# Keeping a V tile whole, and not half of it, in SBUF between two attentions, with half-slot passing of weights and x added by a matmul

## The chip, the cores and the metric

One core of one Trainium2 chip runs the kernel; the other cores are idle. The metric is the device time of one execution in microseconds (us). "Time" below is the median of several executions. The "span" of a profile is shorter (180.4 us where the time was 182.13 us), because the time also holds start and end of the execution. PE is the matrix engine (TensorE), DVE the vector engine, ACT the scalar engine, POOL GpSimd.

## The reference, cut to what matters

Two attention layers and two feed-forward layers alternate, and both attentions use the same weights and the same caches:

```python
x = A_x                                                     # 4 x 1 x 512
x = x + _A_ref(_layernorm(x), A_k_cache, A_v_cache, A_wq, A_wo)
x = x + _B_ref(_layernorm(x), B_w_gate, B_w_up, B_w_down)
x = x + _A_ref(_layernorm(x), A_k_cache, A_v_cache, A_wq, A_wo)
x = x + _B_ref(_layernorm(x), B_w_gate, B_w_up, B_w_down)
# _A_ref: 32 query heads, 8 kv heads of 128, batch 4, softmax over the last
#         2048 of 8192 cache positions
# _B_ref: sigmoid(x @ w_gate) * (x @ w_up) @ w_down, hidden size 1792
```

All data is bf16. One V tile of 1 MiB holds the window of one kv head for two of the four batches, so there are 16 V tiles. SBUF cannot hold everything until the second attention, so most V tiles, the q weights and the feed-forward weights are read again. What stays need not be read.

## The kernel before: the parts that matter here

SBUF is an arena of slots; a 1-MiB tile takes two neighbouring slots, a half tile takes one. All big transfers are issued by one engine (SyncE, "SPq" in the profile) in one fixed order. Each is issued when its slot is free: from a pool, or from a fixed "home", a half slot of a tile that has been used up. `done` marks the last use of a tile and starts whatever transfer can then go.

```python
homes = {}; hfree = set(); on_free = {}
X = ("V", HKV - 2, 1, 0)        # kv head 6, batch pair 1, first layer
Y = ("V", HKV - 1, 0, 0)
Z = ("V", HKV - 1, 1, 0)
GA = ("wg", 0, 0)               # the gate tiles of the first feed-forward
GB = ("wg", 1, 0)

def can_take():
    name = loads[0][0]
    if name in homes:
        return all(n in base for n, _ in homes[name]) and hfree.issuperset(home(name))
    return bool(pool.free)

def done(name):
    left[name] -= 1
    if left[name] == 0:
        s = where.pop(name)
        if name in on_free: on_free[name](s)
        else:               pool.release(s)
        fill()              # issue what can go now
# ... cut ...
def load_v(h, bp, k, n_use):
    name = ("V", h, bp, k)
    if k == 1 and (h, bp) == (HKV - 2, 1):      # only its second half is read again
        load_half(name, pair_d(A_v, h, bp)[:, :, SLOT:2 * SLOT], "bw_4k", SLOT, (X, 1))
        del on_free[name]
        return
    load(name, n_use, "bw_8k", (2 * SLOT, pair_d(A_v, h, bp), True))
    if k == 1 and (h, bp) == (HKV - 2, 0):
        homes[name] = [(Y, 0), (Y, 1)]
```

`pair_d(A_v, h, bp)` is the window of one V tile in HBM. `load_half` fills one slot with rows of 4096 B, `load` two slots. In the second attention the heads run from 7 down to 0. The order of the big transfers around it is: up and down weights of the first feed-forward, the q weights once more, the half V tile, V(6,0), V(5,1), V(5,0), and so on. I call V(6,0), V(5,1) and V(5,0) the **first, second and third V tile of the second attention**. V(7,0) and a half of V(7,1) wait in PSUM in between ("stash").

## Time and profile before

| what | value | read as |
|---|---|---|
| time | 182.08 us (181.89 to 182.09, 3 runs) | |
| span of the profile | 180.4 us | |
| DVE busy | 58% | no compute engine is near the bound |
| PE busy | 56% | |
| ACT, POOL busy | 18%, 12% | |
| big transfer queue | 71.31 MB, 96.7% of 16 engines | the transfers nearly fill the span |

Sixteen transfer engines share each transfer, so the row of DMA shares is a mean over them. A mean of 1.0 over 2 us is read as nobody having waited (the share comes out above 1 in places, so small steps in it mean little).

### The profile page before, as it was taken

What the parts mean: (1) busy time and instruction counts of PE and PEld (TensorE: products, weight loads), DVE (VectorE), ACT (ScalarE), POOL (GpSimd) and SP (SyncE); (2) the same over time, 40 slices, a digit from 0 to 9 for tenths busy, and PEclk for the clock granted to TensorE, in tenths of its full rate; (3) what the DMA queues carried; (4) which work ended last, traced back from release to release, by engine and by line L of the source; (5) the groups of instructions that cost most, each with busy time, mean ns of one, the idle gap of its engine ahead of it and who ended that gap; (6) DMA issues with size and microseconds to landing.
All of it is one profiled execution on the core that took longest, in us unless ns stands there. A gap on an engine that the chain in (4) does not pass through costs nothing.

```text
span 180.4 us, 3873 instructions
## 1 busy us (share of the span) xinstructions
PE 101.6 (56%) x1639; PEld 54.9 (30%) x1651; DVE 104.4 (58%) x257; ACT 32.7 (18%) x87; POOL 21.3 (12%) x86
## 2 busy tenths in 40 slices
PE   0535326572825518335356658354977997667743
PEld 0102111342411514213226542231323443426311
DVE  7208997758474494663745564124589999531431
ACT  2002031221030300302003001001225545410101
POOL 6000010100010100101001000000013435322000
PEclk9999999999999999999999999999999999965555
DMA  5999999999999999999999999999999999999970
GB/s 188 421 429 425 423 423 414 416 423 416 421 414 423 416 423 421 414 420 425 408 420 421 409 403 403 415 352 414 391 400 429 430 412 427 414 414 407 413 312 16
DMA packets 12514, 71.57 MB, mean 397 GB/s; under 512 B 1224, under 2 KB 1232, under 8 KB 6096
## 3 DMA queue, kind: packets, MB, share of 16 engines
q1 hardware_dynamic: 12488, 71.31, 96.7%
q8 instruction: 13, 0.21, 0.5%
q14 instruction: 5, 0.04, 0.1%
q10 hardware_dynamic: 8, 0.00, 0.0%
HBM read 71.31 MB, written 0.00 MB: 395 GB/s over the span
## 4 chain that ended last, share of the span: by engine, by line
DMA 47%; PE 21%; DVE 21%; SPq 4%; ACT 3%; issue 3%; DVEq 0%; ACTq 0%
DMA arena<-in_A_v_cache_dram 31%; DVE arena L818 11%; DMA arena<-in_B_w_down_dram 9%; PE ps L847 8%; DMA arena<-in_A_wq_dram 5%; PE ps L935 5%; SPq L398 4%; PE ps L836 3%; DMA arena<-in_B_w_up_dram 3%; DVE nmax L858 2%; ACT prow L888 1%; ACT prow L873 1%; PE ps L1122 1%; PE ps L1016 1%; DVE ebuf L893 1%
## 5 line engine op out<-in xcount | busy, mean ns | idle before, releaser
L818 DVE STREAM_TRANSPOSE arena<-arena 128x1024 f32<-128x1024 f32 x32 | 37.0, 1203 | 0.0
L847 PE MATMUL ps<-arena,qbd 128*32 128x512 bf16 x256 | 25.8, 539 | 0.0
L935 PE MATMUL ps<-ebuf,arena 128*128 128x8 bf16 x576 | 17.8, 168 | 9.5 <-DMA arena<-in_A_v_cache_dram 5.4
L836 PE MATMUL ps<-msk_m,msk_s 128*32 128x512 bf16 x64 | 8.6, 527 | 23.0 <-DVE arena L818 21.8
L858 DVE TENSOR_REDUCE nmax<-ps 128x1 f32<-128x512 f32 x16 | 10.8, 676 | 17.6 <-PE ps L847 17.6
L935 PEld LDWEIGHTS ps<-ebuf,arena 128*128 128x128 bf16 x576 | 16.8, 104 | 11.6 <-DMA arena<-in_A_v_cache_dram 6.5
L873 ACT ACTIVATE prow<-ps,nmax 128x512 bf16<-128x512 f32 x16 | 11.0, 688 | 35.1 <-DVE nmax L870 29.5
L811 ACT CAST qbd<-ps 128x256 bf16<-128x256 f32 x16 | 5.9, 370 | 44.3 <-PE ps L847 34.8
L759 PE MATMUL ps<-arena,xn 128*4 128x512 bf16 x64 | 8.3, 572 | 6.6 <-DMA arena<-in_A_wq_dram 6.1
L847 PEld LDWEIGHTS ps<-arena,qbd 128*32 128x32 bf16 x256 | 8.5, 122 | 10.7 <-issue 7.8
L902 POOL CAST s<-psm 128x1 bf16<-128x1 f32 x9 | 1.7, 189 | 83.9 <-ACT prow L873 83.9
L888 ACT CAST prow<-ps 128x512 bf16<-128x512 f32 x16 | 9.4, 587 | 10.7 <-PE ps L935 2.1
L893 DVE STREAM_TRANSPOSE ebuf<-prow 128x256 f32<-128x256 f32 x16 | 7.0, 438 | 4.2 <-ACT prow L888 4.1
L836 PEld LDWEIGHTS ps<-msk_m,msk_s 128*32 128x32 bf16 x64 | 1.8, 101 | 23.8 <-DVE arena L818 19.0
L1288 PE MATMUL ps<-arena,xn 128*4 128x448 bf16 x64 | 7.2, 559 | 3.3 <-DMA arena<-in_B_w_up_dram 2.3
L1016 PE MATMUL ps<-arena,ebuf 128*32 128x512 bf16 x112 | 8.1, 413 | 1.2 <-DMA arena<-in_A_v_cache_dram 1.0
L772 DVE STREAM_TRANSPOSE ebuf<-ps 128x512 f32<-128x512 f32 x3 | 2.2, 718 | 11.2 <-PE ps L759 11.1
L806 PE MATMUL ps<-qh,eyew 32*128 32x64 bf16 x64 | 5.6, 217 | 5.0 <-ACT qbd L811 2.4
L737 ACT ACTIVATE lnv<-ps 128x4 f32<-128x4 f32 x4 | 0.7, 174 | 41.7 <-PE ps L733 41.7
L943 DVE TENSOR_TENSOR onb<-ps,rinv 128x16 bf16<-128x16 f32 x9 | 1.7, 185 | 10.7 <-PE ps L935 10.7
L1122 PE MATMUL ps<-onp,arena 128*128 128x16 bf16 x144 | 5.3, 175 | 2.4 <-DVE onp L958 2.4
L1026 DVE STREAM_TRANSPOSE arena<-ps 128x512 f32<-128x512 f32 x7 | 4.8, 692 | 2.8 <-PE ps L1016 2.8
(107 smaller groups left out, 128.1 us busy)
## 6 DMA issues: line engine op xcount, KB each, us to landing
arena<-in_A_v_cache_dram SPq DMA_DIRECT2D x29, 1024.0 KB, 21.2
arena<-in_A_k_cache_dram SPq DMA_DIRECT2D x16, 1024.0 KB, 25.2
arena<-in_A_wq_dram SPq DMA_DIRECT2D x6, 1024.0 KB, 9.3
arena<-in_A_wo_dram SPq DMA_DIRECT2D x4, 1024.0 KB, 25.0
arena<-in_B_w_gate_dram SPq DMA_DIRECT2D x4, 896.0 KB, 17.3
arena<-in_A_wq_dram SPq DMA_DIRECT2D x4, 512.0 KB, 9.3
arena<-in_B_w_up_dram SPq DMA_DIRECT2D x4, 448.0 KB, 7.1
arena<-in_B_w_up_dram SPq DMA_DIRECT2D x2, 896.0 KB, 24.2
```

The source lines that it names most:

```text
L398: o = P.op("sync", name, 0.0, lambda e, dst=dst, src=src: e.dma_start(dst, src), r=r, w=w, dma_bytes=nbytes, dma_rate=tm[rate])
L759: last = pe.matmul(ps[32 * hh:32 * hh + NB, qb, :], xn[:, c * NB:(c + 1) * NB], src[:, o + hh * 512:o + (hh + 1) * 512], start=(c == 0), s ...
L818: P.op("vector", "T%d_%d" % (h, t), c_dve(1024), lambda v, v32=v32: v.transpose(v32, v32), r=[("slot", 4 * h + t)], w=[("slot", 4 * h + t)])
L836: last = pe.matmul(ps[32 * gi:32 * gi + 32, bank, :], msk_s[:, :], msk_m[:, :].unsqueeze(1).broadcast_to([128, 256, 2]), start=True, stop= ...
L847: last = pe.matmul(ps[32 * gi:32 * gi + 32, bank, :], qbd[:, q0:q0 + 32], kt[:, cp // 2, cp % 2, jh * NJ:(jh + 1) * NJ, :], start=False, s ...
L858: lambda v: v.tensor_reduce(nmax[:, k2:k2 + 1], ps[:, bank, :], AXX, ALU.max),
L873: lambda a: a.activation(prow[:, :].rearrange("p (m x t) -> p m x t", x=32, t=2), ps[:, bank, :].rearrange("p (m t x) -> p m x t", x=32, t ...
L888: P.op("scalar", "pc" + tag, c_act(512), lambda a: a.copy(prow[:, :], ps[:, pb, :]), r=[("ppb", pb)], w=[("prow",)], banks=(pb,))
L893: P.op("vector", "pt" + tag, c_dve(256), lambda v: v.transpose(et, prow[:, :].bitcast(F32)), r=[("prow",)], w=[("e", k2)])
L935: last = pe.matmul(ps[:, ob, bp * 8:bp * 8 + 8], src[:, j * 128:(j + 1) * 128], ev[:, j % 2, j % 16 // 2, x0:x0 + 8], start=(j == 0), stop ...
L1016: last = pe.matmul(ps[32 * g:32 * g + 32, ob, :], ew[:, g, mq, t], src.rearrange("p (m t d) -> p t m d", t=2, d=128)[:, t], start=(n == 0) ...
L1288: last = pe.matmul(ps[32 * g:32 * g + NB, gub[n], 0:NF], xn[:, c * NB:(c + 1) * NB], slot_ap(s)[:, g * NF:(g + 1) * NF], start=(c == 0), s ...
```

## The change

The intent is to read 512 KB less. The other half of V(6,1) stays too, so nothing of that tile is read again. The price is room: one slot fewer is free in the feed-forward part. So the homes are shared out anew: the gate tiles GA and GB give their room in halves, the down weights come in four pieces (three of 512 KB, one of 256 KB), and the q weights go where gate tiles and V(7,0) were. The core of the diff (`...` marks what is cut):

```diff
-        X = ("V", HKV - 2, 1, 0)
...
-                    load_half(("wq", c, k), ..., ((X, 1), (Y, 0), (Y, 1), (Z, 0))[c])
+                    load_half(("wq", c, k), ..., ((Y, 1), (Z, 0), (GA, 0), (GA, 1))[c])
...
-                    homes[name] = [((GA, GB)[cc], 0), ((GA, GB)[cc], 1)]
+                    homes[name] = [((GB, Y)[cc], 0), ((GB, Y)[cc], 1)]
...
-                        load_half((nm, c, k), src[:, c, :], "bw_3k", F, ((X, 1), (Y, 0), (Y, 1), (Z, 0))[c])
+                        load_half((nm, c, k), src[:, c, :], "bw_3k", F, ((Y, 0), (Y, 1), (Z, 0), (GA, 0))[c])
...
-            if k == 1 and (h, bp) == (HKV - 2, 1):
-                load_half(name, pair_d(A_v, h, bp)[:, :, SLOT:2 * SLOT], "bw_4k", SLOT, (X, 1))
-                del on_free[name]
-                return
             load(name, n_use, "bw_8k", (2 * SLOT, pair_d(A_v, h, bp), True))
             if k == 1 and (h, bp) == (HKV - 2, 0):
-                homes[name] = [(Y, 0), (Y, 1)]
+                homes[name] = [(GA, 0), (GA, 1)]
...
+        stay = keep[1:] + [(HKV - 2, 1)]
```

Further parts: the input x is put into the PSUM bank of the wo sums by one fp32 matmul with an identity (before, DVE added it after the sum); eight q matmuls go in front of the first scores of the second attention (`score(0, lambda: q_mms(1, 0, OBS[1], (0, 1)))`); in the last attention unit one group of wo matmuls moves and the sums use another bank.

## The prediction

> **What bounds the kernel now.** I read four views of the kernel before, in this order. First the page's slices, because a kernel that streams 71 MB once is suspected of being limited by its transfers (each character or number is one fortieth of the span, 4.51 us):
>
> ```profile
> DMA  5999999999999999999999999999999999999970
> GB/s 188 421 429 425 423 423 414 416 423 416 421 414 423 416 423 421 414 420 425 408 420 421 409 403 403 415 352 414 391 400 429 430 412 427 414 414 407 413 312 16
> ...
> q1 hardware_dynamic: 12488, 71.31, 96.7%
> ```
>
> The reader is to see that the transfer engines are busy in every slice but the first and the last two, at 403 to 430 GB/s with two dips (352 and 391, slices 27 and 29). No compute row is near that (the page gives DVE 58% and PE 56%). Second, the chain of work that ended last:
>
> ```profile
> DMA 47%; PE 21%; DVE 21%; SPq 4%; ACT 3%; issue 3%; DVEq 0%; ACTq 0%
> ```
>
> DMA has the largest share but not all of it, because the chain walks from a transfer back to the compute that freed its room. So the third question is whether the room comes in time. The trace has for each transfer the time of its issue and of its landing. Before each issue between 80 and 135 us there were still 3 to 6 transfers in flight, worth 3.9 us or more of streaming: the half V tile went out at 120.67 us when the transfer before it landed at 128.75; the next V tile but one at 128.52 us against 132.69. A transfer on an idle queue took 4.98 us to land (first wq tile, 0.79 to 5.77 us), of which 1 MiB at the later spacing of landings, 2.48 us, leaves about 2.5 us of lead. So the waits of the queue for compute (27.6 us in the longest group of the view of the queue's own waits) cost nothing: they are the throttle of a full pipe. The two dips aren't starvation either: in windows of 2 us the transfer engines stay busy while the packets become slow.
>
> ```profile
> 116.00:118.00 2.00, 0.68 (x23) 0.60 (x24) 0.00 (x0) 0.00 (x0) 0.00 (x0) 1.00 1.03 377
> 118.00:120.00 2.00, 1.20 (x25) 1.03 (x22) 0.60 (x4) 0.00 (x0) 0.00 (x0) 1.00 0.96 307
> 120.00:122.00 2.00, 1.50 (x10) 0.59 (x10) 0.36 (x2) 0.00 (x0) 0.00 (x0) 1.00 1.02 414
> ```
>
> The last two columns are the DMA share and GB/s. Fourth, the timeline of the end, to see whether transfers or compute set it:
>
> ```profile
> 170.76 0.92 PE L1288 MATMUL ps<-arena,xn 128*4 128x448 bf16 x8
> ...
> 173.01 0.92 PE L1288 MATMUL ps<-arena,xn 128*4 128x448 bf16 x8 [1.33 <-DMA arena<-in_B_w_up_dram]
> ...
> 175.47 1.02 PE L1331 MATMUL ps<-arena,hT 128*4 128x128 bf16 x32 [1.12 <-DMA arena<-in_B_w_down_dram]
> 176.70 1.02 PE L1331 MATMUL ps<-arena,hT 128*4 128x128 bf16 x24 [0.20 <-DMA arena<-in_B_w_down_dram]
> ```
>
> In the last feed-forward part PE waits 1.33 us for the second up tile, then for each down tile; the last lands at 177.29 us, and the 3.1 us from there to the end of the span (last matmuls, casts, store) are fixed. So the time is: start of the stream, bytes over rate, fixed tail.
>
> **What the Trainium skill says.** "DMA: Bandwidth & Descriptors", section "Where 436 GB/s comes from", puts the fabric's ceiling at 435 GB/s; the slices here top out at 430, so there is no idle bandwidth to win, only bytes. The same page's "Rules for kernel authors" ask for 1 MiB per DMA. Half slots break that rule, but with several transfers queued the trace shows little harm: a packet of 8192 B took 311 ns in the median, one of 4096 B 159 ns, one of 6144 B 239, one of 2048 B 84. "TensorE: Matmul & The Clock Gate", "What's actually happening", says that an array that was not busy lately runs at half clock; the trace agrees: the 16 score matmuls took 1.92 us at 126.55 us and 1.11 us at 137.46. "PSUM — Partial Sum Buffer", "The four PSUM rules", says that only the first matmul of a group may clear the bits that make the others accumulate; that fits the diff, in which x's matmul opens the bank and the first wo matmul no longer does. No time follows from it.
>
> **The change, part by part.** I compared instruction order and waits of both programs on every engine.
>
> (1) The half V tile (512 KB) of the second attention is no longer read: 128 rows of 4096 B over 16 engines are 8 packets each, 8 x 159 ns = 1.27 us. The same from the rate: 0.524 MB / 414 GB/s = 1.27 us. This is on the path, since the pipe is full.
>
> (2) The down weights' third piece (768 KB, rows of 6144 B) becomes 512 KB and 256 KB: 159 + 84 - 239 = 4 ns a row, 8 rows an engine, +0.03 us. The number of transfers is the same.
>
> (3) Room comes later for several transfers. Putting the times of the kernel before on the new releasers: the third up tile now waits for the second stash transpose, about 106.9 us (issued at 104.74 before), where the transfer ahead of it lands at 111.05; the fourth for the first gate matmuls, about 108.9, against 112.19; the last wq tile for the first matmuls on the new q weights, about 120.7, against some 126; the next V tile for the third group of those, about 124.2, against some 128.7; the next for q matmuls at about 127, against some 131. The smallest lead is 3.3 us, above the 2.5. Cost 0.
>
> (4) x by a matmul. One GpSimd select and one fp32 matmul go in front of the first q matmuls. They wait for the select, about 6.8 us in place of 5.81; the first two groups of 1.02 us together still end before the second wq tile is there (8.25 us). Cost 0. In return the addition after the reduce (0.18 us, DVE) goes; but the gate matmuls after it wait for the second gate tile (landed 108.81) anyway. Gain 0.
>
> (5) Second attention. The two halves put aside in PSUM come back (2 x 0.73 us) while the last q weights are still streaming, not after; that is no longer in front of the first scores. Instead eight q matmuls (about 1.0 us at the slow clock) go in front of them and wait for a wq tile that landed at 126.13. I get the first scores at 127.2 us where they were at 126.55, the second scores at 130.1 (129.96), and the transpose of the first probabilities at 133.15 (132.89): compute runs 0.3 us later through the second attention. It has slack: the up wait above is 1.33 us. With the second up tile 1.24 us earlier (171.73) and PE free at 171.68 + 0.3, hT is ready at about 173.9, and the first down tile lands at 174.2. Cost 0.
>
> (6) In the last unit the sums move to another bank and one group of wo matmuls moves back in order, so the first PV half need not wait for a reciprocal (162.65 us). The path there is the GpSimd product ending at 163.42, so gain 0.
>
> Sum: -1.27 + 0.03 = -1.24 us, 182.08 - 1.24 = 180.84, rounded to **180.8 us** (-0.7%).
>
> **The rivals.** (A) Compute of the second attention becomes the bound, and part of the gain stays in a shorter wait. For it: its units follow one another every 3.3 us without waiting for V tiles until 153.96 us, and my working leaves 0.3 us of slack at the first down tile. Against: behind that tile lies more slack, because the three groups of down matmuls need 1.8 us and are spread over 2.3 by their tiles; compute must be about 1.1 us late to cost anything. At its likely worst, another 0.5 us: 181.3. (B) The queue starves in the feed-forward part, as a whole slot less is free there. For it: the lead of 3.3 us is the smallest of the kernel, and one engine may run ahead of the others. Against: the rate at the smallest leads of before (4 transfers in flight at 104 us) was 404 GB/s, no dip. It would cost up to 1 us: 181.8. (C) The dips (about 1 us of bytes together, worked out from the windows) come from the order of the transfers and change with it. They have no releaser, so I can't tell which way: 180.0 to 181.7. (D) The bytes are hidden anyway and nothing is gained, 182.1: I see no place in which the pipe is empty, so unlikely.
>
> **Range and chances.** The centre is 180.8. (C) and the spread of the runs (181.89 to 182.09) give 0.5 either way; (A) and (B) only lengthen, so the range is 180.2 to 181.5. Faster by over 2% means under 178.4 us, which needs twice the bytes saved: 0.01. Slower by over 2% means over 185.7, which needs a starved queue of 5 us: 0.01. Within 2%: 0.98.
>
> **What would show it right or wrong.** Right: bytes of the big queue fall to 70.8 MB, slices stay at 400 to 430 GB/s through the feed-forward part, the last down tile lands near 176.05 us, and the wait for the second up tile shrinks from 1.33 us to almost nothing (step 5). Step 3 is wrong if a new dip comes with a DMA share under 0.9 between 108 and 135 us. Step 5 is wrong if the down matmuls wait for hT and not for a transfer. Step 4 is wrong if a q matmul before 10 us starts after its tile by more than it does now. The whole is wrong if the stream is as long as before with fewer bytes.

## The result

The changed kernel took **182.08 us** (181.92 to 182.33, 4 runs), the kernel before in the same rounds 181.99 us (181.41 to 182.09, 4 runs). The outputs are right. The ratio is 1.0013, with a 95% interval of 0.9988 to 1.0037. A ratio is the mean time of one kernel's runs over that of the other's of the same rounds, so it is not quite the ratio of the medians quoted. The 0.52 MB are gone and the time is the same; the prediction of 180.8 us (180.2 to 181.5) missed.

The page of the kernel after, in the slices of one fortieth of the span, the big queue, and the engines' shares of the chain that ended last:

```profile
DMA  5999999999999999999999999999999999999970
GB/s 192 416 429 427 422 425 411 416 422 420 420 414 424 414 424 420 416 416 424 412 417 427 406 402 384 411 331 420 369 393 418 424 425 420 418 411 404 418 292 11
...
q1 hardware_dynamic: 12488, 70.79, 96.5%
...
DMA 36%; DVE 32%; PE 21%; SPq 4%; issue 3%; ACT 2%; POOL 1%; DVEq 0%; ACTq 0%
```

The bytes fell as foreseen, from 71.31 to 70.79 MB. The share of the queue hardly moved, so the packets of fewer bytes took nearly as long. The slices 25, 27 and 29 fell from 403 to 384, from 352 to 331 and from 391 to 369 GB/s. Transfers lost 11 points of the chain to DVE, and the chain through DVE is work whose end frees room for a transfer.

The timeline of the end in the kernel after (start and duration in us, then the releaser and the idle time before):

```profile
170.56 0.92 PE L1295 MATMUL ps<-arena,xn 128*4 128x448 bf16 x8 [0.82 <-DMA arena<-in_B_w_up_dram]
172.83 0.92 PE L1295 MATMUL ps<-arena,xn 128*4 128x448 bf16 x8 [1.35 <-DMA arena<-in_B_w_up_dram]
...
175.32 1.02 PE L1338 MATMUL ps<-arena,hT 128*4 128x128 bf16 x32 [1.14 <-DMA arena<-in_B_w_down_dram]
176.57 1.01 PE L1338 MATMUL ps<-arena,hT 128*4 128x128 bf16 x24 [0.23 <-DMA arena<-in_B_w_down_dram]
```

It is the picture of before, 0.1 to 0.2 us earlier: PE still waits 1.35 us for the second up tile, and then for the down tiles. So compute is not the bound. The last landing came at nearly the same time (177.16 us against 177.29), though the stream had less to carry: it must have been slower, or idle, somewhere.

The windows of 2 us at the entry of the second attention show where. First the kernel before, then the kernel after (the window, its length, busy time and count for PE, PE weight loads, DVE, ACT and POOL, the granted clock, the DMA share, GB/s):

```profile
126.00:128.00 2.00, 1.85 (x20) 0.68 (x20) 0.81 (x2) 0.26 (x1) 0.00 (x0) 1.00 1.04 406
128.00:130.00 2.00, 2.00 (x28) 0.69 (x24) 1.34 (x5) 0.37 (x1) 0.00 (x0) 1.00 1.03 412
130.00:132.00 2.00, 1.88 (x20) 0.52 (x13) 2.00 (x5) 0.78 (x2) 0.00 (x0) 1.00 0.93 348
132.00:134.00 2.00, 1.83 (x32) 0.72 (x32) 1.50 (x3) 0.86 (x2) 0.54 (x2) 1.00 1.00 418
```

```profile
118.00:120.00 2.00, 1.15 (x14) 0.91 (x14) 0.80 (x6) 0.00 (x0) 0.00 (x0) 1.00 1.04 274
...
126.00:128.00 2.00, 2.00 (x24) 0.81 (x27) 0.00 (x0) 0.37 (x1) 0.00 (x0) 1.00 1.09 387
128.00:130.00 2.00, 2.00 (x24) 0.56 (x16) 0.56 (x1) 0.25 (x1) 0.00 (x0) 1.00 0.94 369
130.00:132.00 2.00, 2.00 (x20) 0.44 (x16) 1.86 (x7) 0.91 (x3) 0.00 (x0) 1.00 0.85 344
132.00:134.00 2.00, 1.42 (x28) 0.67 (x29) 1.90 (x5) 0.86 (x2) 0.54 (x2) 1.00 0.97 401
```

From 126 to 134 us the kernel before moved 406, 412, 348 and 418 GB/s, the kernel after 387, 369, 344 and 401. That is 83 GB/s less over 2 us, or 0.17 MB of the 0.52 MB saved. Between 130 and 132 us the DMA share is 0.85: engines were idle, which is the sign that the prediction had named for its step 3. Already before, that window had 0.93, which the prediction did not look at; but a second trace of the kernel before (run e6_before_again) has no dip there:

```profile
130.00:132.00 2.00, 1.39 (x28) 0.59 (x21) 1.97 (x5) 1.17 (x3) 0.00 (x0) 1.00 1.00 401
```

The changed kernel shows it in both its traces (0.89 and 356 GB/s in e0_after_again). The dip at 118 to 120 us (307 GB/s before, 274 after) has a share of 0.96 and 1.04, so there the packets were slow and almost nobody waited.

### The profile page after: what moved, and what is told of

Read it like the earlier page. It is cut to its first block, busy times and chain, and to the rows that moved or that the text cites. A ratio compares the mean times of both kernels' runs of the same rounds, so it can differ in the third digit from the quotient of the medians.

```text
span 180.3 us, 3876 instructions
## 1 busy us (share of the span) xinstructions
PE 101.7 (56%) x1641; PEld 54.9 (30%) x1653; DVE 104.3 (58%) x256; ACT 32.7 (18%) x87; POOL 21.5 (12%) x87
## 3 DMA queue, kind: packets, MB, share of 16 engines
q1 hardware_dynamic: 12488, 70.79, 96.5%
## 4 chain that ended last, share of the span: by engine, by line
DMA 36%; DVE 32%; PE 21%; SPq 4%; issue 3%; ACT 2%; POOL 1%; DVEq 0%; ACTq 0%
DMA arena<-in_A_v_cache_dram 20%; DVE arena L819 11%; DMA arena<-in_B_w_down_dram 9%; PE ps L848 7%; DMA arena<-in_A_wq_dram 5%; PE ps L938 5%; DVE nmax L861 4%; SPq L398 4%; DMA arena<-in_B_w_up_dram 2%; PE ps L837 2%; DVE arena L1027 2%; DVE ebuf L896 2%; DVE nmax L865 2%; DVE mxt L869 2%; DVE arena L1032 1%
## 5 line engine op out<-in xcount | busy, mean ns | idle before, releaser
L1019 PE MATMUL ps<-arena,ebuf 128*32 128x512 bf16 x112 | 7.5, 385 | 0.2 <-DVE nmax L873 0.2
L1306 DVE STREAM_TRANSPOSE ebuf<-ps 128x448 f32<-128x448 f32 x4 | 2.6, 651 | 7.1 <-PE ps L1295 7.1
```

Source lines behind the costliest of these rows:

```text
L1019: last = pe.matmul(ps[32 * g:32 * g + 32, ob, :], ew[:, g, mq, t], src.rearrange("p (m t d) -> p t m d", t=2, d=128)[:, t], start=(n == 0) ...
```

## Reading the stream engine by engine

A mean share does not tell which engines wait. The trace has sixteen completions for each transfer, one of each engine. From these I worked out, for each transfer, the time between one completion and the next, place by place in the order of arrival (first engine with first engine, and so on). For the second V tile of the second attention, which takes 2.48 us an engine in a full pipe, in us:

```
before   3.20 3.16 3.09 3.08 3.04 2.98 2.90 2.88 2.57 2.93 2.48 2.48 2.49 2.49 2.48 2.46
after    3.05 2.92 2.94 2.93 2.91 3.01 2.79 2.79 2.76 2.74 2.69 2.79 2.76 3.09 3.21 3.36
```

In the kernel before the first ten places lost up to 0.7 us on this tile, and the six last lost nothing. The landing, which is the last engine's, showed a clean 2.5 us. So in this execution the stage was already short of work before the change, and the view by landings hid it. In the second trace of the same kernel the loss is small (2.57 us in the mean, 2.76 at most): the kernel before stood at the edge.

The reason is that the sixteen engines are not in step. In the kernel before, the first transfers of the program arrive on all engines within 0.39 us. In the transfer that streams from 30 to 34 us the spread becomes 1.53 us, and it does not close again (1.4 to 3.0 us from there to the end). At 30.8 us the trace has one packet of 16,384 B of the instruction queue, which took 1.08 us on one engine. This fits the size of the jump; the profile does not say which engine carried it. The trace of the kernel before has thirteen such packets of 0.88 to 1.11 us, and the five 1-MiB tiles that stream when one is carried at 43.5, 59.8, 72.1, 85.7 and 99.0 us took 2.57 to 2.60 us in the mean of the engines, the other 1-MiB tiles in rows of 8192 B of that stretch 2.45 to 2.52. My estimate from these numbers, 2.49 us plus a sixteenth of 1.08, is 2.56.

**The account.** The mean completion over the sixteen engines is a steadier clock for the account than the last one, though the time itself follows the last: in all 14 traces the profiled execution took 4.83 to 4.95 us more than its last landing. Three things came out of the mean. (a) From the end of the third V tile of the second attention on, the rest of the stream took 38.56 to 38.74 us in all 14 traces, so everything is decided before. (b) The last big transfer completed at 175.53 us (mean of engines) in the kernel before, at 175.60 in a second trace of it, and at 175.14, 174.91 and 175.22 us in three traces of the changed kernel or one of the same order of transfers. That is 0.48 us earlier in the mean, where 1.27 were removed. (c) The three V tiles together took 7.83 and 7.63 us before and 8.37, 8.34 and 8.40 after, which is 0.64 us more. The last up piece took 1.13 and 1.15 us before and 1.34, 1.34 and 1.21 after, 0.16 us more. The down pieces of the first feed-forward took 4.47 and 4.88 us before and 4.54, 4.53 and 4.81 after, so 0.05 us less in the mean, which is nothing beside their scatter. And -1.27 + 0.64 + 0.16 - 0.05 = -0.52, near the measured -0.48. So 0.8 us of the 1.27 were lost in two places, and the larger is the entry of the second attention.

## The experiments

Three theories went into the runs. **S**: at the entry of the second attention the transfers wait for compute to free their room; the engines that are ahead run dry, and removing bytes in front of such a wait only makes the wait longer. **P**: the loss is in slow packets (as at 118 us) and in the chance of which engine ends last. **C**: compute is the bound. The runs came in three calls, each on another chip; those of one call share the runs of the kernel before. Its times were 181.61 us (181.06 to 182.53, 11 runs) in the first call, 182.0 (181.61 to 182.84, 11) in the second and 181.83 (181.32 to 182.45, 11) in the third.

| run | time, us (range, runs) | ratio to before [95%] | three V tiles, us | mean end of stream, us |
|---|---|---|---|---|
| e6_before_again | 181.76 (181.37 to 182.01, 4) | 0.9978 [0.9948, 1.0007] | 7.63 | 175.60 |
| e0_after_again | 181.3 (181.07 to 182.97, 6) | 1.000 [0.996, 1.0039] | 8.34 | 174.91 |
| e1_bytes_alone | 181.87 (181.54 to 182.35, 6) | 1.001 [0.9983, 1.0038] | 8.77 | 174.90 |
| e2_more_room | 180.56 (180.17 to 181.13, 6) | 0.9938 [0.991, 0.9965] | 7.55 | 173.75 |
| e2_more_room_again | 180.44 (180.25 to 180.84, 4) | 0.9917 [0.989, 0.9944] | 7.61 | 174.16 |
| e7_room_and_bytes | 181.74 (181.56 to 182.46, 6) | 0.9988 [0.996, 1.0015] | 7.54 | 175.20 |
| e3_bytes_back | 182.21 (181.47 to 182.85, 6) | 1.0025 [0.9993, 1.0057] | 7.62 | 176.29 |
| e4_halves | 181.13 (180.3 to 181.76, 6) | 0.9943 [0.9914, 0.9971] | 8.32 | 174.58 |
| e4_halves_again | 181.3 (180.44 to 181.53, 6) | 0.9958 [0.9934, 0.9982] | 7.92 | 174.51 |
| e8_more_halves | 180.97 (180.38 to 181.97, 6) | 0.9958 [0.9927, 0.9988] | 7.80 | 174.51 |
| e5_scores_first | 181.52 (180.97 to 182.85, 6) | 0.998 [0.9945, 1.0015] | 8.14 | 174.87 |
| e9_x_by_vector | 181.76 (181.17 to 182.63, 4) | 0.9997 [0.9965, 1.0028] | 8.40 | 175.22 |

The last two columns are of the one profiled execution of each run, the times of all.

### The same kernels again: what a run scatters

No edit in either: e0 is the changed kernel, e6 the kernel before.

> The changed kernel unaltered, for a second trace and a tighter interval. Theory S (starved queue: with less room the transfers into the second attention are issued too late, so the engines idle and the saved 1.27 us are lost there): 181.7 to 182.3 us, with idle of the DMA engines again between 130 and 135 us and again between 110 and 115. Theory P (packets happened to be slow in the one trace, at 117 to 120 and 126 to 128 us, and one engine lagged at the end): the median comes nearer to 181.3 and the slow spells move or vanish in the second trace.

> The kernel before unaltered, for a second trace. All theories: ratio 1.00 within 0.4%. Theory S: again some idle between 130 and 135 us, about 0.2 us an engine, less than the changed kernel has.

The changed kernel gave 1.000, the unchanged one 0.9978 against itself. The median of the changed kernel, 181.3 us, is the figure that P had named, but the kernel before was faster in this call too (181.61), so the ratio counts, and it shows no gain. The idle of S is there again (a share of 0.89 from 130 to 132 us). So a single ratio of some six runs is good to about 0.3% or 0.5 us, and the missing gain of 0.7% is more than that. The account by engines, which does not depend on the end, is steadier: the three V tiles took 8.37 and 8.34 us in the two traces of the changed kernel.

### The bytes alone

The kernel before, with the load of the half V tile replaced by nothing. Half of V(6,1) is then stale, so the result is wrong, though within the tolerance.

```diff
-                load_half(name, pair_d(A_v, h, bp)[:, :, SLOT:2 * SLOT], "bw_4k", SLOT, (X, 1))
-                del on_free[name]
+                left[name] = 1
+                homes[name] = [(X, 1)]
+                loads.append((name, lambda s: None))
```

> The kernel before with the half V tile simply not read (wrong result on purpose, everything else as before). If the stream is bound by bytes, it is 1.27 us faster: 180.7. Theory S: the next V tile but one is still issued when the first scores are done, about 128.5 us, and the tile ahead of it now lands about 131.4, a lead of 2.9 us for its last engine and under 1 us for its first; the engines idle there and only 0.2 to 0.8 us are gained, 181.2 to 181.8. Theory P: 180.7 or what the slow packets leave.

The ratio was 1.001 [0.9983, 1.0038]: with everything else as before, 512 KB less in the stream gained nothing that these runs can see, where 0.7% was the price of the bytes. S had expected 0.2 to 0.8 us of gain. The windows of this run:

```profile
126.00:128.00 2.00, 1.73 (x20) 0.70 (x20) 0.93 (x2) 0.37 (x1) 0.00 (x0) 1.00 1.06 420
128.00:130.00 2.00, 2.00 (x32) 0.75 (x28) 1.24 (x4) 0.37 (x1) 0.00 (x0) 1.00 0.69 289
130.00:132.00 2.00, 1.67 (x29) 0.49 (x18) 1.98 (x5) 1.25 (x3) 0.00 (x0) 1.00 0.82 311
132.00:134.00 2.00, 1.56 (x30) 0.53 (x22) 1.86 (x6) 0.39 (x2) 0.53 (x2) 1.00 0.97 381
```

The DMA share falls to 0.69 and 0.82. Here the idle time stands in the open: the second V tile was issued at 128.64 us, as in the kernel before (128.52), because its room is freed by score matmuls, and those do not come sooner for there being fewer bytes. The first engine had done with the first V tile at 129.20 us, 0.6 us after that issue. The second tile then took 4.12 us in the first place of the order of arrival in place of 2.48, and 2.77 in the last. In the mean the three tiles took 8.77 us against 7.73, so 1.04 of the 1.27 us was lost there. This is S in its plainest form. (The stream of this trace still ended 0.7 us earlier than before, because the q weights ahead took 10.44 us and not 10.92; the traced execution, 181.56 us, was nearly the fastest of the six, whose median was 181.87.)

### More room, the same bytes

The changed kernel, but V(6,1) is not kept, nor read again: V(6,0) is used in its place, so the result is wrong. The slots that V(6,1) held go to the pool. The first V tile takes those, and the second V tile takes the home that the first had.

```diff
-            if k == 1 and (h, bp) == (HKV - 2, 0):
+            if k == 1 and (h, bp) == (HKV - 3, 1):
                 homes[name] = [(GA, 0), (GA, 1)]
...
-        stay = keep[1:] + [(HKV - 2, 1)]
+        stay = keep[1:]
...
+            if h == HKV - 2:
+                v_tiles[(2, h)] = [(bp, ("V", h, 0, 1)) for bp in range(2)[::-1]]
...
-                if (h, bp) not in keep + stay:
-                    load_v(h, bp, 1, 1)
+                if (h, bp) not in keep + stay + [(HKV - 2, 1)]:
+                    load_v(h, bp, 1, 2 if (h, bp) == (HKV - 2, 0) else 1)
```

> The changed kernel with its bytes but one whole slot more room: the second V tile of head 6 isn't kept (its place goes to the pool, and the second attention reads the other tile twice; wrong result on purpose). V tiles are issued one slot earlier. Theory S: the idle at 130 to 135 us vanishes, 0.4 to 1.0 us faster than the changed kernel, 181.1 to 181.7. Theory P: no difference to the changed kernel beyond 0.2 us.

> The same kernel as e2_more_room, to see how far a ratio moves from call to call, and to set e4_halves and e8_more_halves beside the kernel that has room in plenty on the same chip. Theory S: ratio 0.992 to 0.995, the best of this call or equal to e8_more_halves. Theory P: ratios of all kernels move toward 1.0.

The ratios were 0.9938 and 0.9917. With the bytes of the changed kernel and two slots more, the gain is there: the mean of the two is 0.9928, or 1.3 us of 182, about the 1.24 us predicted and more than S had expected (181.1 to 181.7 us; it was 180.56). The two V tiles went out at 120.64 and 123.97 us in place of 124.68 and 127.73. The windows of the first of these runs:

```profile
126.00:128.00 2.00, 2.00 (x24) 0.66 (x20) 0.97 (x2) 0.00 (x0) 0.00 (x0) 1.00 1.07 438
128.00:130.00 2.00, 2.00 (x28) 0.61 (x24) 2.00 (x4) 0.37 (x1) 0.00 (x0) 1.00 0.99 414
130.00:132.00 2.00, 0.73 (x13) 0.18 (x5) 1.76 (x9) 0.78 (x2) 0.00 (x0) 1.00 1.01 418
132.00:134.00 2.00, 2.00 (x33) 0.73 (x32) 1.42 (x4) 1.46 (x4) 0.53 (x2) 1.00 1.02 422
```

The dip is gone, 414 to 438 GB/s throughout, and the second V tile took 2.47 to 2.50 us in every place. The gain lies where S puts it: the streams of the two traces ended 1.1 us before those of the changed order in the mean, 0.8 us of it on the three V tiles and 0.2 on the q weights ahead, while the last up piece (1.30 and 1.23 us) was as slow as without the room. The dip in that place in the first trace of the kernel before was the same shortage, by its share of 0.93 and its late first engines; the prediction had taken it for slow packets and for something without a releaser. In the changed kernel part of the loss shows as slow packets and not as idle time (369 GB/s at a share of 0.94, 387 at 1.09); these vanish too when there is room, so they go with the thin queue. How, the traces do not tell.

### More room and the bytes back

The kernel of the last experiment, and half of V(7,1) is read once more into the place where it already is, just ahead of the V tiles.

```diff
+                if (h, bp) == (HKV - 2, 1):
+                    loads.append((("K", "again"), lambda _: dma(
+                        "again", slot_ap(base[Z] + 1), pair_d(A_v, HKV - 1, 1)[:, :, SLOT:2 * SLOT],
+                        w=[("slot", base[Z] + 1)], rate="bw_4k")))
```

> The kernel with a slot more room (wrong result on purpose) and in it 512 KB read again, in 4096-byte packets, into a place that holds them already, just before the V tiles of the second attention. Theory S: with room there is no idle to hide the bytes, so they cost their whole 1.27 us over the kernel with room: 181.8 against 180.56. If they cost much less, the stream isn't what sets the time even with room, and the theory is short of something.

The ratio was 0.9988, 0.6% (1.1 us) above the mean of the two runs with room. These ratios come from different calls. In the traces the mean end of the stream came at 175.20 us against 173.75 and 174.16, so 1.25 us later. Where the room comes in time, 512 KB cost what the packets say, 1.27 us. Where it does not, taking them out gains next to nothing, as the run with the bytes alone showed. The price of the bytes was right; it is only due where the pipe is full.

### The bytes back, in the changed kernel

The changed kernel, with the second half of V(6,1) read again into its own place ahead of the first V tile.

```diff
-            if name in (Y, Z, GA, GB):
+            if name in (Y, Z, GA, GB, ("V", HKV - 2, 1, 0)):
...
+                if (h, bp) == (HKV - 2, 1):
+                    loads.append((("K", "again"), lambda _: dma(
+                        "again", slot_ap(base["V", HKV - 2, 1, 0] + 1), pair_d(A_v, HKV - 2, 1)[:, :, SLOT:2 * SLOT],
+                        w=[("slot", base["V", HKV - 2, 1, 0] + 1)], rate="bw_4k")))
```

> The changed kernel, and the half V tile is read again from memory into the place where it already lies (right result), at the point of the stream where the kernel before read it. If the stream is bound by bytes: 1.27 us slower than the changed kernel, 183.3. Theory S: the added 512 KB fill time in which the engines would have idled, so it costs 0.3 to 0.8 us, 182.4 to 182.9. Theory P: 183.3.

The ratio was 1.0025 [0.9993, 1.0057]. The changed kernel twice and one of the same order of transfers (the last experiment) gave 1.0013, 1.000 and 0.9997, so the bytes cost about 0.2%, or 0.4 us, with an interval of about 0.6 us either way. The trace is half with S: the first two tiles took 2.48 and 2.55 us, so the extra transfer did fill the gap. But this one trace also lost time elsewhere (0.2 us on the last up piece, 0.3 on the extra transfer itself, and slow packets between 121 and 125 us), and its stream ended 1.2 us later in the mean. The run does not decide.

### Issuing by halves

If S holds, the changed kernel can be mended without giving up its saving: the first two V tiles go out as two transfers of 512 KB each, each as soon as its half slot is free. The result is right. The core of the edit:

```diff
+                on_free["wq", (0, 0), k] = lambda s: hfree.add(s + 1)
...
+            if k == 1 and (h, bp) in ((HKV - 2, 0), (HKV - 3, 1)):
+                pair = GA if h == HKV - 2 else GB
+                for n in range(2):
+                    load_half(name if n else name + ("a",), pair_d(A_v, h, bp)[:, :, n * SLOT:(n + 1) * SLOT], "bw_4k", SLOT, (pair, n))
+                on_free[name] = lambda s: pool.release(s - 1)
+                return
...
+                if name == ("wq", (0, 0), 1) and c == 0:
+                    give(s)          # the first half slot, after the first four q matmuls
```

> The changed kernel, right result, same bytes, but the first two V tiles of the second attention come as two transfers of 512 KB each into the two halves of the same places, so that each half is issued when its own half is free (after the third and the fourth group of q matmuls, and after each of the two groups in front of the first scores) and not when both are. Theory S (the queue starves at the entry of the second attention): the first engine has about 4 us of lead in place of 2.8 before the first tile and 2.8 in place of 2.3 before the second; idle between 130 and 135 us falls by at least half, and the kernel is 0.4 to 0.8 us faster than the changed one. Theory P (slow packets by chance): no difference, or 0.05 us slower for the smaller packets.

> The same kernel as e4_halves, for a second call of its own and to stand beside e8_more_halves. Theory S: ratio to the kernel before 0.994 again, within 0.002. Theory P: the gain was partly luck of the call, the ratio anywhere from 0.994 to 1.0.

The ratios were 0.9943 and 0.9958; both intervals end below 1. This kernel is 0.5% or 0.9 us faster than the kernel before, and by the three ratios of the changed order (mean 1.0003) also faster than that, a little more than S had expected (0.4 to 0.8 us). In the second run the windows were these:

```profile
126.00:128.00 2.00, 1.98 (x20) 0.83 (x24) 0.00 (x0) 0.37 (x1) 0.00 (x0) 1.00 1.04 408
128.00:130.00 2.00, 2.00 (x24) 0.66 (x16) 0.45 (x1) 0.14 (x1) 0.00 (x0) 1.00 1.01 401
130.00:132.00 2.00, 1.40 (x20) 0.34 (x16) 1.86 (x7) 1.01 (x3) 0.00 (x0) 1.00 1.04 375
132.00:134.00 2.00, 1.23 (x20) 0.59 (x25) 1.90 (x5) 0.86 (x2) 0.53 (x2) 1.00 1.03 408
```

The share is above 1.0 in all four, but the rate is 375 to 408, below the kernel with more room: nobody idles, some packets are still slow. The first run shows the opposite:

```profile
130.00:132.00 2.00, 1.31 (x20) 0.52 (x13) 1.93 (x6) 0.88 (x3) 0.00 (x0) 1.00 0.83 307
```

There the expectation of S, that the idle falls by at least half, missed: the second tile took 3.16 us in the mean, and the three tiles 8.32, hardly less than in the changed kernel (8.37). Yet its stream ended as early as that of the second run. Against the changed order the two streams ended 0.5 us earlier in the mean, 0.25 us of it on the V tiles and as much on the q weights ahead of them (10.65 and 10.76 us against 10.96). So the gain in time is shown twice; that all of it comes from the earlier V halves is not.

### One half more

The first 1 MiB of the last q weights is cut in two as well, so that the first q matmuls could start on a half.

```diff
...
-                for cc in range(NC // 2):
-                    name = ("wq", (0, cc), k)
-                    load(name, 2, "bw_4k", (2 * SLOT, wq_d[:, 2 * cc:2 * cc + 2, 0:SLOT], False))
-                    homes[name] = [((GB, Y)[cc], 0), ((GB, Y)[cc], 1)]
+                for c in range(2):
+                    load_half(("wq", (0, c), k), wq_d[:, c, 0:SLOT], "bw_4k", SLOT, (GB, c))
+                name = ("wq", (0, 2), k)
+                load(name, 2, "bw_4k", (2 * SLOT, wq_d[:, 2:4, 0:SLOT], False))
+                homes[name] = [(Y, 0), (Y, 1)]
...
```

> e4_halves with one more transfer cut in two: the first 1 MiB of the last q weights as two of 512 KB, each issued as its half slot comes free, so the first q matmuls (which free the room of the second V tile read in this stage) wait for the first half alone. Result right. Theory S (the engines that are ahead run dry at the entry of the second attention): e4_halves still left 0.33 us idle and 0.51 us of slow packets an engine between 123 and 137 us; the second V tile's first half goes out 1 us earlier or more, so part of that goes: 0.2 to 0.4 us faster than e4_halves in the same call, ratio to the kernel before 0.992 to 0.994. Theory P (chance of the slowest engine at the end): the same as e4_halves. Theory C (compute is the bound): the same as e4_halves too, with the down matmuls waiting for hT and not for a transfer.

The ratio was 0.9958, the same as that of e4_halves_again. The expectation of S missed, and the trace says why: the half landed 1.3 us sooner, at 125.38 us, but the second V tile was issued at 127.40 us where it was 127.41. The timeline of PE in this run:

```profile
126.02 0.37 PE L812 MATMUL ps<-qh,eyew 32*128 32x64 bf16 x4 [1.28 <-DVE qh L782]
126.31 0.62 PE L842 MATMUL ps<-msk_m,msk_s 128*32 128x512 bf16 x4
126.71 1.07 PE L765 MATMUL ps<-arena,xn 128*4 128x512 bf16 x8
```

The eight q matmuls that free the room start at 126.71 us (126.72 in the run without this cut). They do not wait for their tile; PE comes to them in its order, behind the first query, for which it waits 1.28 us for DVE. So this edit did not change the lead, and the run says nothing for or against S, only that the next thing to move is the order on PE.

### The scores first

The changed kernel with its eight q matmuls behind the first scores again, as before the change.

```diff
-            score(0, lambda: q_mms(1, 0, OBS[1], (0, 1)))
+            score(0)
             qx(1)
+            q_mms(1, 0, OBS[1], (0, 1))
```

> The changed kernel with the order of the kernel before in one place: the first scores go before the two groups of q matmuls, not after. The second V tile is then released by the scores, later than the 127.7 us of the changed kernel. Theory S: its lead falls to 2 us or less for the last-but-early engines, so more idle, 0 to 0.5 us slower than the changed kernel. Theory C (compute of the second attention is the bound, and the q matmuls in front delay it): 0.2 to 0.5 us faster.

The ratio was 0.998, which tells it apart neither from the kernel before nor from the changed one. The first tile took 2.51 us in place of 2.76, the third 2.88 in place of 2.69, and the stream ended as in the changed kernel. The second V tile went out 0.5 us later, with 1.75 us to the first engine, and took 2.75 us in place of 2.92. The waits change places more than they grow: S had expected 0 to 0.5 us of loss, C 0.2 to 0.5 of gain, and this run decides for neither.

### x on the vector engine

The changed kernel without the matmul for x: the select and the fp32 matmul are gone, the first wo matmul opens the bank again and DVE adds x after the reduce.

```diff
-            P.op("gpsimd", "idx", 500.0, ...)
-            P.op("tensor", "xfold", tm["pe_f32"], ...)
-                wo_unit(tag, h, op, h % 2, False, h == HKV - 1)
+                wo_unit(tag, h, op, h % 2, h == 0, h == HKV - 1)
-            if L == 0:
-                P.op("vector", "xr%d" % L, ...)
-                return
```

> The changed kernel with its fourth part alone taken back: no GpSimd select and no fp32 matmul for x, the first wo matmul opens the bank, and the addition of x after the reduce is back on the vector engine. All theories here: this part has no time, as predicted: the same as the changed kernel, ratio to the kernel before 0.998 to 1.003. If instead part of the missing gain had been lost there, this kernel would be 0.3 us or more faster than the changed one (ratio 0.998 or less).

The ratio was 0.9997 against 1.0013 and 1.000 with the matmul: this part has no time that can be seen, as predicted. Its trace also serves as a third of the changed order of transfers.

## Why the prediction was wrong, point by point

**Step 3 failed: "The smallest lead is 3.3 us, above the 2.5. Cost 0."** The issue times were foreseen well: the first V tile about 124.2 us (measured 124.68), the second at about 127 (127.73). So were the landings ahead of them: some 128.7 and some 131 us (129.06 and 131.73). The measured leads so reckoned, 4.4 and 4.0 us, look ample. But they count to the last of sixteen engines. The first engine was through with the transfer ahead at 127.44 and at 130.02 us, so its leads were 2.8 and 2.3 us. What a lead must cover can be read from the tiles that went dry, as the first engine's completion, less 2.48 us of streaming, less the issue: 2.2 us in the run of the bytes alone, 2.9 and 3.1 for the second tile in the two traces of the changed kernel, and 2.1 for the first transfer of the program. The leads of the two tiles, 2.8 and 2.3 us, left nothing over. Over all runs, the first two V tiles took 2.46 to 2.60 us in the mean where the first engine's lead was 3.3 us or more, and 2.55 to 3.53 us where it was 2.8 or less (tiles in halves counted whole). It is no sharp threshold, and smaller pieces do with less: 448-KB up pieces lost nothing at a lead of 2.1 us, and one 0.2 us at 1.3. The Trainium skill, page "DMA: Bandwidth & Descriptors", section "Why a DMA increments its semaphore by 16 and not by 1", says that the engines of one transfer finish independently; traces agree, with 1.6 to 2.2 us between the first and the last in this stage. I had this in the trace and used only the last completion.

**The reading of the bound, "the throttle of a full pipe", was too broad.** It was true for most of the stream. It wasn't at 130 to 132 us, where the share of the kernel before was 0.93 in the trace that the prediction had, and its first engines had a lead of 2.1 us. The prediction showed the windows from 116 to 122 us, whose dip has indeed a share of about 1.0, and took the second dip, in the slice from 126 to 131 us, for the same thing.

**Step 1** priced the bytes right (1.27 us; about 1.25 in the traces where there is room) but put them "on the path, since the pipe is full". In front of a transfer that waits for compute they are not on the path: bytes removed there shorten the lead of the next one.

**Step 2** (0.03 us for the split down piece) is below what the traces resolve (4.47 and 4.88 us before, 4.54, 4.53 and 4.81 after). **Step 4** was right: the fp32 matmul came at 6.78 us (6.8 foreseen), as this timeline of the kernel after shows, and the q matmuls behind it at 7.31 us, still before the second wq tile:

```profile
6.78 0.61 PE L695 MATMUL ps<-xT,ebuf 128*128 128x16 f32 x2 [1.57 <-POOL ebuf L691]
...
7.31 1.90 PE L760 MATMUL ps<-arena,xn 128*4 128x512 bf16 x16
```

By its letter the sign named for step 4 came true all the same: the first q matmuls now start 1.65 us after their tile, where it was 0.04. The step had foreseen that itself, and it costs nothing, because PE waits for the next tile again (until 10.71 us, 10.76 before).

**Step 5** was right in kind, though the sign that it named, a wait for the second up tile that shrinks to almost nothing, did not come (1.35 us), since the stream was not earlier: the first scores began at 127.47 us (127.2 foreseen), the second at 130.18 (130.1), and the first transpose of probabilities at 133.35 (133.15). Compute ran a little later, and the down matmuls still waited for their tiles and not for hT. **Step 6** was not tested by itself; with PE waiting for the up tile it had nothing to give, and the traces show nothing against that.

**The rivals.** D, "The bytes are hidden anyway", named the outcome, and was put aside with "I see no place in which the pipe is empty". B, starving because "one engine may run ahead of the others", named the mechanism with its right size ("up to 1 us") but in the feed-forward part; there, the last up piece lost 0.16 us with a lead of 1.3 us to the first engine. Its larger part lay at the entry of the second attention, 0.64 us. A, compute as the bound, is refuted by the waits for tiles at the end. C, chance of the dips, plays at 118 to 120 us, but before and after did not differ in it on average: the six transfers of q weights that stream there took 10.93 and 10.92 us before, 11.03, 10.85 and 11.00 after. Over all 14 traces they took 10.44 to 11.22 us, so this stage scatters, over executions and kernels, by nearly as much as the short leads cost.

Two small slips of the working: 3.7 us, which "faster by over 2%" needs, are three times the 1.27 us and not twice, and slice 30, at 400 GB/s, lies below the "403 to 430" read from the page. Neither bears on the result.

**What stays open.** The traces of the changed order account for a stream 0.5 us shorter than before, while the timed ratios (1.0013, 1.000, 0.9997) show no gain. A difference of 0.3 to 0.5 us is at the edge of what these runs can tell. Part of it is which executions were traced: 181.18 and 181.17 us in two of the three traces of the changed order are near the lower ends of their ranges (181.07 to 182.97, 181.17 to 182.63), while the two traced executions of the kernel before (182.13 and 181.87) lie above their medians (182.08 and 181.76). And part is the last engine, which sets the time: in the first trace of the changed kernel it ended 2.02 us behind the mean, in the others 1.10 and 1.41, before 1.76 and 1.42. What remains is not settled. The cause of the slow packets at 118 to 120 us, which are in all traces, is open too.

## What to carry to other kernels

In a kernel bound by one stream, ask of each transfer how long before the *first* engine runs dry it is issued, and not before the transfer ahead has landed; sixteen engines that are 2 us apart, as here, make a lead of 4 us one of 2. Bytes removed just ahead of a transfer that waits for compute to free its room gained nothing here until that room came sooner, so buy the room first: two slots more gave the whole 1.3 us, and with the transfers cut in halves that go out as each half slot frees the kernel was 0.9 us faster. A dip of the transfer rate is worth windows of 2 us, in two traces: a share clearly under 1.0 was waiting here and had a releaser, a share of 1.0 was slow packets.

## What the Trainium skill lacked or had wrong

- "DMA: Bandwidth & Descriptors", "Why a DMA increments its semaphore by 16 and not by 1", says that engines finish independently, but not by how much: 0.39 us at the start of this kernel, 1.4 to 3.0 us from 34 us on. Nor does it draw the rule that a lead counts from the first completion (2.1 to 3.1 us were needed for 1-MiB tiles here). No page says that a fetch of instructions holds up one engine of a data stream; here the jump came with a 16,384 B packet of 1.08 us, and thirteen such packets are in each trace.
- The same page, "Rules for kernel authors", asks for 1 MiB per DMA or more for maximum bandwidth. It has no word on a place whose room frees in halves: there two transfers of 512 KB each were faster (0.9943 and 0.9958 against 1.0003 in ratios to the kernel before).
- The same page, "Where 436 GB/s comes from", says that the memory side (about 358 GB/s, the rate of a stack over two cores) binds for reads from HBM. That does not hold for a core that streams alone: here it moved 403 to 430 GB/s in most slices. The same section has 425 GB/s for 16 MB, so it is this sentence, and not the section as a whole, that misleads.
